# A copy moved earlier, two shortcuts at the seam between transform and MLP, a table negation deferred, and halved output tiles, in a fused Fourier-filter and MLP kernel

## The chip, the cores and the metric

The kernel runs on one core of a Trainium2 chip. The metric is the device time of one execution in microseconds (us); lower is better. The traced span (first to last instruction of the profile) is about 2 us shorter than that time, and both are given where it matters.

The engines are named as in the profile: PE is TensorE (matmuls and transposes), DVE is VectorE, ACT is ScalarE, POOL is GpSimd, SP is SyncE, which only issues transfers here.

Some words recur. An eviction copies a matmul's result out of PSUM, where TensorE leaves it, into an ordinary on-chip tile. A spill stores such a tile to the chip's main memory, and a reload brings it back. A transfer lands when its last semaphore event arrives. A launch in which two pieces of work happen to collide is called unlucky.

## The reference

```python
# x: (8, 3008, 256), filt_r and filt_i: (1505, 256)
X = np.fft.rfft(x, axis=1)
Y = X * (filt_r + 1j * filt_i)
y = np.fft.irfft(Y, n=3008, axis=1)          # 8 * 3008 = 24064 rows of 256
h = y.reshape(24064, 256) @ w_in             # w_in: (256, 2048)
g = h / (1 + np.exp(-beta * h))              # Swish with a beta for each column
out = g @ w_out                              # w_out: (2048, 256)
```

## The kernel before

The 3008 rows are split as 47 times 64, so that each transform becomes small matmuls with tables of sines and cosines. Tables `t2` (forward, second stage), `t3` and `t3b` (backward) are computed on the chip at the start. Batch 0 is transformed first, in what this text calls the head (0 to 40 us). Then the MLP starts with 752 steps, each of two 512-column matmuls into `hps`, a Swish on ScalarE and four 256-column matmuls into `acc`. The transforms of batches 1 to 7 are cut into units, and a plan places them between the steps.

These are the parts that the change touches. First the table copies in the head, issued on VectorE in program order after the evictions of column groups 3 and 4:

```python
def t2_more(h, eng):
    ks_ = slice(h * NH, (h + 1) * NH)
    nc.vector.tensor_scalar_mul(t2[:, ks_, 4, :], t2[:, ks_, 1, :], -1.0)
    eng.tensor_copy(t2[:, ks_, 3, :], t2[:, ks_, 2, :])
    eng.tensor_copy(t2[:, ks_, 0, :], t2[:, ks_, 1, :])
...
for i in range(3, 5):
    first1(i, (False, False))        # two VectorE evictions each
    warm(2)                          # two matmuls on zeros, the warm-ups
t2_more(0, nc.vector)
```

GpSimd meanwhile computes the second half of the angles: `u`, then `r` (the rounding), then `u - r` (the subtraction).

Next the product with the filter, once for each of 12 pairs of frequencies, and the backward stage of that pair. `fri` is the filter as it arrives by transfers in three groups: pairs 0 to 2, 3 to 5, and 6 to 11.

```python
def product(i):
    ...                                            # forward matmuls into ps
    for dst, ps in zip((p_t, q_t), pss):
        nc.vector.tensor_tensor(dst[:], ps[:], fri[:, 2*i : 2*i+2, :], ALU.mult)

def inverse3(i):
    ...
    last = i == NK // 2 - 1
    one = opsum.tile([P, 2, NDC, P], F32, name="psz", tag="acc")
    two = fpsum.tile([P, 2, NDC, P], F32, name="psz", tag="f") if last else one
    for e, ps in ((0, one), (1, two)):
        ...                                        # matmuls with t3 and t3b
    for e0, e1, ps in ((0, 1, one), (1, 2, two)) if last else ((0, 2, one),):
        evac(z_t[...], ps[...], e0 == 0)           # ScalarE, then VectorE
```

Then the seam: `z` is transposed (`pz`), the last stage makes `y`, and the first MLP matmul reads 512 columns of `y`. The columns are not in the natural order but in classes of `JG` = 8 residues, `CLS` = 94 * 8 = 752 columns each:

```python
def last_z(g, i, on_act, own=None):
    jq, dc = divmod(i, NDC)
    yv = ys[0][:, dc, g*CLS : (g+1)*CLS].rearrange("p (n j) -> p n j", j=JG)
    return last4(zz0[g], t4b, 4*jq, dc, yv[:, :, 4*jq : 4*jq+4], on_act, own)
...
nc.vector.tensor_scalar_mul(t3[M:P], t3b[M:P], -1.0)   # the table for batches 1 to 7
```

Last, the output: one tile of 4 x 256 columns for each block of 16 steps, two such tiles in the pool.

```python
ost = ostp.tile([P, 4, D], F32, name="ost", tag="ost")
for h, a in enumerate(acc):
    ...
    evac(ost[:, n*h : n*(h+1), :], a[:], on_act)
```

Of the kernel before, what the change touches and what calls it, by code (L numbers as in the profile page):

```python
# [9 lines left out]
P = 128  # L10
# [3 lines left out]
F32 = mybir.dt.float32  # L14
BF16 = mybir.dt.bfloat16
# [16 lines left out]
NJG = J // JG  # L32
VLAG = 3
# [3 lines left out]
def kernel(  # L37
# [23 lines left out]
    CLS = NP * JG  # L61
# [18 lines left out]
    ostp = pool("ostp", 2)  # L80
# [13 lines left out]
    t3 = consts.tile([P, NK, P], BF16, name="t3", tag="t3")  # L94
    ident = consts.tile([P, P], BF16, name="ident", tag="ident")
# [83 lines left out]
    t3b = setup.tile([P, NK, P], BF16, name="t3b", tag="t3b")  # L179
# [191 lines left out]
    for i in range(3, 5):  # L371
        first1(i, (False, False))
        warm(2)
    t2_more(0, nc.vector)
    first1(5, (True, True))
# [70 lines left out]
    def inverse3(i):  # L446
        k0 = 2 * i
        p_t, q_t = pq.pop(i)

        last = i == NK // 2 - 1  # L450
        one = opsum.tile([P, 2, NDC, P], F32, name="psz", tag="acc")
        two = fpsum.tile([P, 2, NDC, P], F32, name="psz", tag="f") if last else one
        for e, ps in ((0, one), (1, two)):
            for src, tab in ((p_t, t3), (q_t, t3b)):
                for dc in range(NDC):
                    nc.tensor.matmul(  # L456
                        ps[:, e, dc, :],
                        lhsT=src[:, e, dc * P : (dc + 1) * P],
                        rhs=tab[:, k0 + e, :],
                        start=src is p_t and dc == 0 and (e == 0 or last),  # L460
                        stop=src is q_t,
                        skip_group_check=True,
                    )
        for e0, e1, ps in ((0, 1, one), (1, 2, two)) if last else ((0, 2, one),):
            evac(
                z_t[:, :, :, 4 * (k0 + e0) : 4 * (k0 + e1)].rearrange(
                    "p c j (e a) -> p e (c j) a", a=4
                ),
                ps[:, e0:e1].rearrange("p e c (j a) -> p e (c j) a", a=4),
                e0 == 0,  # L470
            )
# [49 lines left out]

    def turn_z(g, i, on_act=False):
# [10 lines left out]
    def last4(zz, tab, jj, dc, dst, on_act, own=None):  # L533
# [10 lines left out]
        for n0, n1 in ((0, NP),) if own is None else ((0, TB // JG), (TB // JG, NP)):  # L544
# [11 lines left out]
    def last_z(g, i, on_act, own=None):  # L556
        jq, dc = divmod(i, NDC)
        yv = ys[0][:, dc, g * CLS : (g + 1) * CLS].rearrange("p (n j) -> p n j", j=JG)
        return last4(zz0[g], t4b, 4 * jq, dc, yv[:, :, 4 * jq : 4 * jq + 4], on_act, own)
# [13 lines left out]
    warm(2)  # L573
    rest = []
    for i in range(2 * NDC):
# [4 lines left out]
        if i == 1:  # L580
            warm(2)
    for go in rest:
        go()


    nc.vector.tensor_scalar_mul(t3[M:P], t3b[M:P], -1.0)
# [145 lines left out]

    def ux(b):
# [10 lines left out]
    if B > 1:  # L744
        at = place(1, 11, u1(1, True), per=2)
        place(at + 1, at + 1, [lambda: a2_read(1)] + uf(), per=9)
        at = place(25, 56, u23(1), per=2)
# [18 lines left out]
    def store(t0, tn, ost, eng=nc.sync):  # L766
# [5 lines left out]
        for tb in range(tn // P):  # L772
            c0 = t0 + tb * P
            c1 = c0 + P
            while c0 < c1:
                lo = (c0 - t0) % P
                if c0 >= S:
# [7 lines left out]
                        out.offset + (r // JG * J + g * JG) * D,  # L785
                        [[J * D, n // JG], [D, JG], [1, D]],
# [7 lines left out]
    for s in range(len(steps) + LAG):  # L794
        if s < len(steps):
# [5 lines left out]
            while pos < t0 + tn:  # L801
                b, n0 = divmod(pos, S)
                ln = min(S - n0, t0 + tn - pos)
                for dc in range(NDC):
# [16 lines left out]
        if s >= LAG:  # L821
# [26 lines left out]
            if fb == NFB - 1:  # L848
                ost = ostp.tile([P, 4, D], F32, name="ost", tag="ost")
                for h, a in enumerate(acc):  # L850
                    n = a.shape[1]
                    on_act = h == 0 and i < 6 or last and h % 2 == 0
                    evac(ost[:, n * h : n * (h + 1), :], a[:], on_act)
                    if last:
                        store(t0 + h * P, P, ost[:, h:, :], (nc.sync, nc.scalar)[h // 2])
                if not last:
                    store(t0, tn, ost)
# [30 lines left out]
```

## Time and profile before

| | before |
|---|---|
| time, median of the first 3 runs (range) | 792.48 us (791.69 to 793.87) |
| traced span | 789.8 us |
| TensorE busy | 776.7 us, 98% |
| VectorE, ScalarE, GpSimd busy | 50%, 76%, 18% |
| one MLP step in the steady state | 0.87 us |

The page of the kernel before, parts 1 and 5. Part 1 has the busy us, the share of the span and the number of instructions; part 5 has line, engine, operation, output and input, then busy us, mean ns, and idle time ahead of the group with its main releaser.

```profile
PE 776.7 (98%) x6104; PEld 547.6 (69%) x6104; DVE 396.3 (50%) x644; ACT 596.9 (76%) x920; POOL 144.6 (18%) x143
L840 PE MATMUL acc<-wout_sb,gT 128*128 128x256 bf16 x3008 | 455.1, 272 | 1.2 <-ACT ost L105 0.2
L805 PE MATMUL hps<-y,win_sb 128*128 128x512 bf16 (+7 forms) x1728 | 447.7, 351 | 0.3 <-DVE y L109 0.3
```

TensorE idles only 1.2 and 0.3 us ahead of the MLP's own matmuls. From 43 us on it is back to back apart from 1.1 us of waits (the waits view).

The head of the kernel before, the timeline of TensorE (start us, length us, engine, line, operation, count, and in brackets the idle time before it and its releaser). `pz` are the transposes of z, `hps` is the first MLP step, `acc` the first output matmuls.

```profile
37.35 1.06 PE L568 MATMUL pz<-ident,z_t 128*96 128x128 bf16 x16 [0.61 <-DVE z_t L107]
...
40.30 1.02 PE L805 MATMUL hps<-y,win_sb 128*128 128x512 bf16 x4 [0.35 <-DVE y L109]
...
42.92 0.38 PE L613 MATMUL ps<-xg,t 94*96 94x512 bf16 x1 [0.21 <-DVE a L107]
43.13 0.60 PE L840 MATMUL acc<-wout_sb,gT 128*128 128x256 bf16 x4
```

The same kernel, the timeline of VectorE: the copies, the first product of pair 6, and the negation.

```profile
13.38 0.35 DVE L290 TENSOR_SCALAR t<-t 128x768 bf16<-128x768 bf16 x1
13.64 0.98 DVE L291 COPY t<-t 128x768 bf16<-128x768 bf16 x1
14.55 1.97 DVE L292 COPY t<-t 128x768 bf16<-128x768 bf16 x1
...
27.98 0.69 DVE L443 TENSOR_TENSOR pb_t<-ps,fri 128x512 bf16<-128x512 f32 x1 [0.22 <-PE pb L396]
...
40.66 1.49 DVE L586 TENSOR_SCALAR t<-t3b 64x3072 bf16<-64x3072 bf16 x1
42.18 0.69 DVE L107 CAST a<-ps 96x512 bf16<-96x512 f32 x1
```

And the timeline of GpSimd for the same stretches.

```profile
11.60 2.81 POOL L270 TENSOR_SCALAR r<-u 128x768 f32<-128x768 f32 x1
14.49 1.80 POOL L271 TENSOR_TENSOR u<-u,r 128x768 f32<-128x768 f32 x1
...
39.44 1.89 POOL L149 TENSOR_TENSOR wout_sb<-frr,rbeta_sb 128x1024 bf16<-128x1024 f32 x1 [3.66 <-DMA frr<-in_moe_w_out_dram]
```

Three readings matter. First, the two copies of 128x768 took 0.98 and 1.97 us, although the negation of the same shape just before them took 0.35. They ended about 0.2 us after GpSimd's `r` (14.41) and its subtraction (16.29). Second, the wait before pair 6 at 27.98 is labelled with a transpose on TensorE, but the instruction also needs the filter; the transfers' semaphore events in the trace show the last of the four large filter loads landing at 27.80, so the filter was the true releaser. Third, the negation of 64x3072 took 1.49 us, ended 0.82 us after GpSimd's multiply (41.33), and held back an eviction.

### The profile page before, as it was taken

What the parts mean: (1) busy time and instruction counts of PE and PEld (TensorE: products, weight loads), DVE (VectorE), ACT (ScalarE), POOL (GpSimd) and SP (SyncE); (2) the same over time, 40 slices, a digit from 0 to 9 for tenths busy, and PEclk for the clock granted to TensorE, in tenths of its full rate; (3) what the DMA queues carried; (4) which work ended last, traced back from release to release, by engine and by line L of the source; (5) the groups of instructions that cost most, each with busy time, mean ns of one, the idle gap of its engine ahead of it and who ended that gap; (6) DMA issues with size and microseconds to landing.
All of it is one profiled execution on the core that took longest, in us unless ns stands there. A gap on an engine that the chain in (4) does not pass through costs nothing.

```text
span 789.8 us, 15387 instructions
## 1 busy us (share of the span) xinstructions
PE 776.7 (98%) x6104; PEld 547.6 (69%) x6104; DVE 396.3 (50%) x644; ACT 596.9 (76%) x920; POOL 144.6 (18%) x143
## 2 busy tenths in 40 slices
PE   7899999999999999999999999999999999999998
PEld 4767667766777667876678766686667766776665
DVE  7946935755537464465534746367452761500101
ACT  5887886886678866788677876778767788677776
POOL 9322510330013200131002310024000340000000
PEclk9999999999999999999999999999999999999999
DMA  9978687116811178011860228412370214010101
GB/s 187 232 193 213 155 212 218 49 67 187 215 45 47 68 200 218 29 68 70 216 181 28 86 97 199 152 36 88 110 222 27 74 68 127 30 52 28 54 27 53
DMA packets 83380, 91.43 MB, mean 116 GB/s; under 512 B 3759, under 2 KB 73537, under 8 KB 82287
## 3 DMA queue, kind: packets, MB, share of 16 engines
q1 hardware_dynamic: 80204, 73.95, 30.5%
q0 software_dynamic: 2816, 16.26, 10.8%
q8 instruction: 47, 0.77, 0.4%
q10 hardware_dynamic: 288, 0.26, 0.1%
q14 instruction: 25, 0.20, 0.1%
HBM read 57.16 MB, written 46.66 MB: 131 GB/s over the span
## 4 chain that ended last, share of the span: by engine, by line
PE 93%; DVE 3%; POOL 2%; issue 1%; ACT 1%; DVEq 0%; ACTq 0%; POOLq 0%
PE acc L840 41%; PE hps L805 40%; PE ps L613 3%; PE ps L536 3%; PE ps L635 2%; PE ps L661 2%; DVE ost L107 1%; PE psz L456 1%; POOL xg L116 0%; POOL r L270 0%; ACT a L105 0%; DVE q_t L650 0%; DVE p_t L646 0%; DVE q_t L647 0%; PE pt L352 0%
## 5 line engine op out<-in xcount | busy, mean ns | idle before, releaser
L814 ACT ACTIVATE gT<-hps,beta_sb 128x512 bf16<-128x512 f32 x752 | 516.8, 687 | 175.3 <-PE hps L805 165.5
L840 PE MATMUL acc<-wout_sb,gT 128*128 128x256 bf16 x3008 | 455.1, 272 | 1.2 <-ACT ost L105 0.2
L805 PE MATMUL hps<-y,win_sb 128*128 128x512 bf16 (+7 forms) x1728 | 447.7, 351 | 0.3 <-DVE y L109 0.3
L840 PEld LDWEIGHTS <-gT 128*128 128x128 bf16 x3008 | 285.3, 98 | 132.7 <-issue 4.7
L805 PEld LDWEIGHTS <-win_sb 128*128 128x128 bf16 x1728 | 164.7, 98 | 24.8 <-issue 0.7
L651 POOL TENSOR_TENSOR v_t<-p_t,q_t 128x512 bf16<-128x512 f32 x84 | 106.7, 1270 | 375.3 <-DVE q_t L650 372.7
L107 DVE COPY ost<-acc 128x512 f32<-128x512 f32 (+1 forms) x88 | 56.2, 677 | 193.6 <-PE acc L840 188.0
L107 DVE CAST a<-ps 96x512 bf16<-96x512 f32 x96 | 65.9, 686 | 85.6 <-PE ps L613 85.6
L109 DVE TENSOR_SCALAR y<-ps 128x376 bf16<-128x376 f32 (+2 forms) x120 | 64.5, 541 | 64.3 <-PE ps L536 64.2
L646 DVE TENSOR_TENSOR p_t<-ps,frr 128x512 f32<-128x512 f32 x84 | 58.1, 691 | 31.8 <-PE ps L635 29.4
L650 DVE TENSOR_TENSOR q_t<-ps,fri 64x512 f32<-64x512 f32 x84 | 58.2, 693 | 1.2
L647 DVE SCALAR_TENSOR_TENSOR q_t<-ps,fri 64x512 f32<-64x512 f32 x84 | 57.4, 684 | 1.1
L536 PEld LDWEIGHTS <-zz 96*128 96x128 bf16 x512 | 35.4, 97 | 29.0
L105 ACT ACTIVATE z<-ps 128x512 bf16<-128x512 f32 x84 | 49.5, 590 | 0.7 <-PE ps L661 0.7
L613 PE MATMUL ps<-xg,t 94*96 94x512 bf16 x112 | 41.9, 381 | 0.2 <-DVE a L107 0.2
L536 PE MATMUL ps<-t,zz 96*128 96x94 bf16 x448 | 36.7, 204 | 0.0
L116 POOL DMA_DIRECT2D xg<-in_x_dram x22 | 12.1, 556 | 114.3 <-PE acc L840 97.7
L661 PE MATMUL ps<-v_t,t 128*128 128x256 bf16 x168 | 32.1, 273 | 0.4 <-DVE q_t L650 0.4
L635 PE MATMUL ps<-a,t 128*128 128x256 bf16 x168 | 32.1, 273 | 0.0
L635 PEld LDWEIGHTS <-t 128*128 128x128 bf16 x168 | 15.8, 98 | 14.6
L613 PEld LDWEIGHTS <-t 94*96 94x96 bf16 x112 | 13.8, 123 | 12.1
L661 PEld LDWEIGHTS <-t 128*128 128x128 bf16 x168 | 15.4, 98 | 8.1 <-DVE q_t L650 0.9
(119 smaller groups left out, 201.0 us busy)
## 6 DMA issues: line engine op xcount, KB each, us to landing
out_dram<-ost SPq DMA_DIRECT2D x40, 512.0 KB, 2.8
d<-a SPq DMA_DIRECT2D x28, 384.0 KB, 4.7
a<-d SPq DMA_DIRECT2D x28, 384.0 KB, 5.8
d<-z SPq DMA_DIRECT2D x28, 384.0 KB, 2.6
zz<-d SPq DMA_DIRECT2D x28, 384.0 KB, 4.8
xg<-in_x_dram POOLq DMA_DIRECT2D x6, 1280.0 KB, 10.2
frr<-in_filt_r_dram SPq DMA_DIRECT2D x12, 256.0 KB, 7.9
out_dram<-ost SPq DMA_DIRECT2D x22, 128.0 KB, 7.1
```

The lines of the kernel that those rows point to most:

```text
L107: nc.vector.tensor_copy(dst, src)
L109: nc.vector.tensor_scalar_mul(dst, src, scale)
L536: nc.tensor.matmul(ps[:, e, :NP], lhsT=zz[:, jj + e, dc * P : (dc + 1) * P], rhs=tab[:], start=True, stop=True,)
L613: nc.tensor.matmul(ps[:KP], lhsT=t1[:], rhs=s["x"][:, 2 * i : 2 * i + 2, :], start=True, stop=True)
L635: nc.tensor.matmul(ps[:, e, :], lhsT=t2[:, k0 + e, 3:5, :].rearrange("p c k -> p (c k)"), rhs=s["a2"][g][:, kk + e, :], start=True, stop=True,
L646: nc.vector.tensor_tensor(p_t[:], ps[:], frr[:, ks_, :], ALU.mult)
L650: nc.vector.tensor_tensor(q_t[:M], ps[M:P], fri[M:P, ks_, :], ALU.mult)
L651: nc.gpsimd.tensor_tensor(v_t[:], p_t[:], q_t[:], ALU.add)
L661: nc.tensor.matmul(ps[:, e, :], lhsT=t3[:, k0 + e, :], rhs=v_t[:, e, :], start=True, stop=True)
L805: nc.tensor.matmul(hps[:, pos - t0 : pos - t0 + ln], lhsT=win_sb[:, dc, fb * P : (fb + 1) * P], rhs=ys[b][:, dc, n0 : n0 + ln], start=(dc ...
L814: nc.scalar.activation(gT[:, :tn], hps[:, :tn], ACT.Silu, scale=beta_sb[:, fb : fb + 1])
L840: nc.tensor.matmul(acc[tb // per][:, tb % per, :], lhsT=gT[:, tb * P : (tb + 1) * P], rhs=wout_sb[:, fb, :], start=(fb == 0 and tb % per = ...
```

## The change

The intent has five parts. **A**: the table copies are issued one step earlier, ahead of GpSimd's subtraction. **B**: the last pair's first columns go through the backward stage first. **C**: batch 0's `y` is kept in classes of 4 residues, so that the first 376 columns of the first MLP step need half of the evictions; three warm-up matmuls go. **D**: the table negation moves into the MLP, in four quarters, and `t3b` must then live in the constants. **E**: output tiles hold two chunks instead of four, three in the pool.

```diff
-    CLS = NP * JG
+    CLS = NP * JC                      # JC = 4                              (C)
-    ostp = pool("ostp", 2)
+    ostp = pool("ostp", 3)             #                                     (E)
+    t3b = consts.tile([P, NK, P], BF16, name="t3b", tag="t3b")   # was in setup (D)

-    for i in range(3, 5):
-        first1(i, (False, False))
-        warm(2)
+    first1(3, (False, False))
+    warm(2)
     t2_more(0, nc.vector)              #                                     (A)
+    first1(4, (False, False))
+    warm(2)

# inverse3                                                                    (B)
+        for j0, j1 in ((0, JG), (JG, J)) if last else ((0, J),):
+            ...                        # a PSUM tile for each group of columns
             for src, tab in ((p_t, t3), (q_t, t3b)):
+                for e in range(2):
                 ...
-                        rhs=tab[:, k0 + e, :],
+                        rhs=tab[:, k0 + e, 4 * j0 : 4 * j1],
+            for e in range(2) if last else (None,):
+                ...
+                evac(dst, src, not last or j0 > 0)   # first columns: VectorE

# last_z                                                                      (C)
-        return last4(zz0[g], t4b, 4*jq, dc, yv[:, :, 4*jq : 4*jq+4], on_act, own)
+        n0 = NP if jq == 0 else (TB - CLS) // JC
+        return last4(zz0[g], t4b, JC * jq, dc, yv, on_act, own, n0)
-    warm(2)
+    warm(1)
-        if i == 1:
-            warm(2)

-    nc.vector.tensor_scalar_mul(t3[M:P], t3b[M:P], -1.0)
...
+        place(14, 20, ut(4), per=2)    # the same in four quarters           (D)

# the first MLP step alone is cut at the class                                (C)
+                if s == 0:
+                    ln = min(ln, CLS - n0 % CLS)

-                ost = ostp.tile([P, 4, D], F32, name="ost", tag="ost")
                 for h, a in enumerate(acc):
+                    if h * per % 2 == 0:
+                        ost = ostp.tile([P, 2, D], F32, name="ost", tag="ost")   # (E)
```

More of the change, by code (lines that the diff above doesn't have):

```diff
@@ L32 @@
 NJG = J // JG
+JC = 4
 VLAG = 3
@@ L177, in bits @@
         return tf
-    t3b = setup.tile([P, NK, P], BF16, name="t3b", tag="t3b")
     wz = setup.tile([P, 512], BF16, name="wz", tag="wz")
@@ L450, in inverse3 @@
         last = i == NK // 2 - 1
-        one = opsum.tile([P, 2, NDC, P], F32, name="psz", tag="acc")
-        two = fpsum.tile([P, 2, NDC, P], F32, name="psz", tag="f") if last else one
-        for e, ps in ((0, one), (1, two)):
-            for src, tab in ((p_t, t3), (q_t, t3b)):
-                for dc in range(NDC):
-                    nc.tensor.matmul(
-                        ps[:, e, dc, :],
-                        lhsT=src[:, e, dc * P : (dc + 1) * P],
-                        rhs=tab[:, k0 + e, :],
-                        start=src is p_t and dc == 0 and (e == 0 or last),
-                        stop=src is q_t,
-                        skip_group_check=True,
-                    )
@@ L464, in inverse3 @@
-        for e0, e1, ps in ((0, 1, one), (1, 2, two)) if last else ((0, 2, one),):
-            evac(
-                z_t[:, :, :, 4 * (k0 + e0) : 4 * (k0 + e1)].rearrange(
-                    "p c j (e a) -> p e (c j) a", a=4
-                ),
-                ps[:, e0:e1].rearrange("p e c (j a) -> p e (c j) a", a=4),
-                e0 == 0,
-            )
+        for j0, j1 in ((0, JG), (JG, J)) if last else ((0, J),):
+            nj = 4 * (j1 - j0)
+            if j0:
+                ps = fpsum.tile([P, 2, NDC, nj], F32, name="psz", tag="f")
+            else:
+                ps = opsum.tile([P, 2, NDC, nj], F32, name="psz", tag="acc")
+            for src, tab in ((p_t, t3), (q_t, t3b)):
+                for e in range(2):
+                    for dc in range(NDC):
+                        nc.tensor.matmul(
+                            ps[:, e, dc, :],
+                            lhsT=src[:, e, dc * P : (dc + 1) * P],
+                            rhs=tab[:, k0 + e, 4 * j0 : 4 * j1],
+                            start=src is p_t and dc == 0 and e == 0,
+                            stop=src is q_t,
+                            skip_group_check=True,
+                        )
+            for e in range(2) if last else (None,):
+                if last:
+                    dst = z_t[:, :, j0:j1, 4 * (k0 + e) : 4 * (k0 + e) + 4]
+                    src = ps[:, e].rearrange("p c (j a) -> p c j a", a=4)
+                else:
+                    dst = z_t[:, :, :, 4 * k0 : 4 * k0 + 8].rearrange(
+                        "p c j (e a) -> p e (c j) a", e=2
+                    )
+                    src = ps.rearrange("p e c (j a) -> p e (c j) a", a=4)
+                evac(dst, src, not last or j0 > 0)
@@ L531, in turn_z, with last4 @@
         evac(zz0[g][:, 4 * i : 4 * i + 4, :], pz[:KP], on_act)
-    def last4(zz, tab, jj, dc, dst, on_act, own=None):
+    def last4(zz, tab, jj, dc, dst, on_act, own=None, first=NP):
         ps = own or fpsum.tile([P, 4, P], F32, name="ps4", tag="f")
@@ L543, in last4 @@
         rest = []
-        for n0, n1 in ((0, NP),) if own is None else ((0, TB // JG), (TB // JG, NP)):
+        for n0, n1 in ((0, NP),) if own is None or first == NP else ((0, first), (first, NP)):
             rest.append(
@@ L557, in last_z @@
         jq, dc = divmod(i, NDC)
-        yv = ys[0][:, dc, g * CLS : (g + 1) * CLS].rearrange("p (n j) -> p n j", j=JG)
-        return last4(zz0[g], t4b, 4 * jq, dc, yv[:, :, 4 * jq : 4 * jq + 4], on_act, own)
+        c = g * JG // JC + jq
+        yv = ys[0][:, dc, c * CLS : (c + 1) * CLS].rearrange("p (n j) -> p n j", j=JC)
+        n0 = NP if jq == 0 else (TB - CLS) // JC
+        return last4(zz0[g], t4b, JC * jq, dc, yv, on_act, own, n0)
     for i in range(4):
@@ L731, in uf, with ut @@
         ]
+    def ut(n):
+        return [
+            lambda k=k: nc.vector.tensor_scalar_mul(
+                t3[M:P, k : k + NK // n], t3b[M:P, k : k + NK // n], -1.0
+            )
+            for k in range(0, NK, NK // n)
+        ]
     def ux(b):
@@ L784, in store @@
                         out.tensor,
-                        out.offset + (r // JG * J + g * JG) * D,
-                        [[J * D, n // JG], [D, JG], [1, D]],
+                        out.offset + (r // JC * J + g * JC) * D,
+                        [[J * D, n // JC], [D, JC], [1, D]],
                     ),
@@ L848 @@
             if fb == NFB - 1:
-                ost = ostp.tile([P, 4, D], F32, name="ost", tag="ost")
                 for h, a in enumerate(acc):
-                    n = a.shape[1]
+                    if h * per % 2 == 0:
+                        ost = ostp.tile([P, 2, D], F32, name="ost", tag="ost")
+                    c = h * per % 2
                     on_act = h == 0 and i < 6 or last and h % 2 == 0
-                    evac(ost[:, n * h : n * (h + 1), :], a[:], on_act)
-                    if last:
-                        store(t0 + h * P, P, ost[:, h:, :], (nc.sync, nc.scalar)[h // 2])
-                if not last:
-                    store(t0, tn, ost)
+                    evac(ost[:, c : c + per, :], a[:], on_act)
+                    eng = nc.scalar if last and h >= 2 else nc.sync
+                    store(t0 + h * per * P, per * P, ost[:, c : c + per, :], eng)
 _INS = ['x', 'filt_r', 'filt_i', 'moe_w_in', 'moe_w_out', 'moe_beta']
```

## The prediction

> **What bounds the kernel now.** The page's busy table gives TensorE 776.7 of 789.8 us (98%). In the timeline, from 43 us on, one MLP step (two 512-column and four 256-column matmuls) repeats every 0.87 us, with side work between; the waits view shows under 1.5 us of TensorE waits after that. So only the head, 0 to 43 us, holds time that this change can win.
>
> **Step A, table copies one step earlier.** VectorE's two 128x768 bf16 copies take 0.98 and 1.97 us (0.35 each in their second half at 24.4 us). They end when GpSimd's ops end (14.41, 16.29). [...] the table negation at 40.66 ends 0.82 us after GpSimd's multiply. TensorE idles 14.4 to 16.66 waiting for these copies. Issued about 1 us earlier, they end at perhaps 13.5 to 14.7, if GpSimd's rounding (11.60 to 14.41) lets them; then up to 2 us are gained at 16.66. But I expect almost none to survive: VectorE's product of pair 6, at 27.98, waits for the four large filter loads, whose last landing in the trace is 27.80. From 27.98 to 36.18 VectorE is busy without a gap. Earlier pairs only wait there. Worth 0 to 0.2 us, estimated.
>
> **Step B, last pair's first columns first.** After the last product (36.18) the transposes start at 37.35, behind a 0.39 us ScalarE and a 0.42 us VectorE eviction of 256 elements. Then VectorE evicts two pieces of 64 elements (0.2 us each, estimated from 0.17 for 16 and 0.28 for 128): transposes at about 37.0. Gain 0.35 us.
>
> **Step C, classes of 4 residues, three fewer warm-up matmuls.** The first MLP matmul (40.30) waits for all four evictions of y, the last at 40.24. Then its 376 columns need only the first two. With 0.54 and 0.48 us for these evictions, the first MLP step ends at about 39.9 instead of 40.73: 0.8 us together with B. The ten extra small matmuls hide in waits.
>
> **Step D, negation moved.** 1.49 us of VectorE at 40.66 leave; they delayed an eviction (42.18) for which TensorE waited 0.38 us at 42.5. The four quarters (about 0.3 us each) fall at 54 to 62 us, where VectorE has idle time. Gain 0.4 us.
>
> **Step E, half output tiles.** Twice the store issues. Reuse distance falls from two blocks to one and a half, about 14 us instead of 28 from eviction to reuse; stores land in 2.8 to 7 us, latest for block 0 (issued at 68 to 72, evicted at 61). 0, with a small risk around 80 us. The tail is unchanged.
>
> **Sum.** Estimated 1.2 us of the head, plus 0 to 0.2 from A: **791.1 us**, range 789.5 to 792.4. Chances: faster by over 2% 0.01, within 2% 0.98, slower by over 2% 0.01.
>
> **What would show it.** A: transposes of the first table well before 16.66, yet VectorE's pair 6 still at about 27.9 with a wait before it of 1 to 2 us. B: transposes of z at about 37.0. C: first MLP matmul at about 39.4, first SiLU at about 40.1 (was 40.93). D: no wait before the third stage-1 matmul after the first steps; from there all MLP steps about 1.2 us earlier, unchanged to the end.
>
> **What would make it wrong.** The big filter loads landing earlier or later (then A counts); the copies still blocked, with two evictions now behind them; transposes waiting for the second column group; an output eviction waiting for a store; run-to-run scatter (2.2 us over three runs of before) is as large as the effect.

0.8 us from B and C and 0.4 us from D make the 1.2 us, with 0 to 0.2 us from A on top.

## The result, and the profile after

| | before | after |
|---|---|---|
| time, median of 6 runs (range) | 792.33 us (791.69 to 793.87) | 790.63 us (790.00 to 792.63) |
| ratio, with its 95% interval | | 0.9978 (0.9964 to 0.9993) |
| traced span | 789.8 us | 788.4 us |
| TensorE busy | 776.7 us | 777.5 us |

A ratio here is the mean time of one kernel's fast runs over that of the kernel before in the same rounds, so it is not quite the ratio of the medians quoted.

The page of the kernel after, part 1 and the same two groups:

```profile
PE 777.5 (99%) x6111; PEld 547.9 (69%) x6111; DVE 394.4 (50%) x647; ACT 597.4 (76%) x920; POOL 144.6 (18%) x143
L860 PE MATMUL acc<-wout_sb,gT 128*128 128x256 bf16 x3008 | 455.1, 272 | 1.2 <-ACT ost L107 0.2
L825 PE MATMUL hps<-y,win_sb 128*128 128x512 bf16 (+8 forms) x1730 | 447.7, 351 | 0.0
```

The MLP itself costs the same 455.1 and 447.7 us. The timeline of TensorE in the head of the kernel after:

```profile
36.06 1.06 PE L581 MATMUL pz<-ident,z_t 128*96 128x128 bf16 x16 [0.19 <-DVE z_t L109]
...
38.26 1.04 PE L825 MATMUL hps<-y,win_sb 128*128 128x376 bf16 x6
...
40.74 0.60 PE L860 MATMUL acc<-wout_sb,gT 128*128 128x256 bf16 x4
```

From the first `pz` to the first `hps` it is now 2.20 us (2.95 before), and the wait before `pz` is 0.19 us (0.61 before). The timeline of VectorE for the kernel after:

```profile
12.36 0.35 DVE L291 TENSOR_SCALAR t<-t 128x768 bf16<-128x768 bf16 x1
12.63 0.35 DVE L292 COPY t<-t 128x768 bf16<-128x768 bf16 x1
12.90 0.35 DVE L293 COPY t<-t 128x768 bf16<-128x768 bf16 x1
...
27.01 0.69 DVE L446 TENSOR_TENSOR pb_t<-ps,fri 128x512 bf16<-128x512 f32 x1 [0.64 <-PE ps L437]
```

The timeline of GpSimd for the kernel after:

```profile
11.61 2.81 POOL L271 TENSOR_SCALAR r<-u 128x768 f32<-128x768 f32 x1
```

The copies now take 0.35 us each, in the middle of GpSimd's `r`. Yet VectorE then stands idle before pair 6 (0.64 us): the filter landed at 26.83, and pair 6 started 0.18 us later. Pair 6 is 0.97 us earlier than in the trace of before, and the first temptation is to credit that to A. The filter loads were not touched by A, though. On the other hand, VectorE itself was ready for pair 6 only at 27.76 in the trace of before (27.98 less 0.22), so with copies held up as there, the earlier landing alone could have gained no more than 0.22 us. The experiments had to say whose gain this was.

The two traces, cut at the same events, add up exactly. Positive numbers are time lost by the kernel after:

| stage | before | after | difference |
|---|---|---|---|
| start of pair 6 | 27.98 | 27.01 | -0.97 |
| pair 6 to the end of the last product | 8.19 | 8.19 | 0 |
| end of products to first transpose of z (B) | 1.18 | 0.86 | -0.32 |
| first transpose of z to first MLP matmul (C) | 2.95 | 2.20 | -0.75 |
| first MLP matmul to first output matmul (D) | 2.83 | 2.48 | -0.35 |
| first output matmul to Swish 4 (counted from 0) | 2.74 | 2.73 | -0.01 |
| Swish 4 to 42 | 42.52 | 42.53 | +0.01 |
| Swish 42 to 52 | 12.06 | 12.30 | +0.24 |
| Swish 52 to 83 | 33.82 | 33.86 | +0.04 |
| Swish 83 to 90 | 6.77 | 7.19 | +0.42 |
| Swish 90 to 751 | 643.60 | 643.59 | -0.01 |
| last Swish to the end | 5.18 | 5.44 | +0.26 |
| sum | 789.82 | 788.39 | -1.43 |

So 2.4 us were gained up to Swish 4, and about 0.95 us were given back later in four places of which the prediction named none.

### The profile page after: what moved, and what is told of

The parts are those of the page before. It is cut to its first block, busy times and chain, and to the rows that moved or that the text cites. A ratio compares the mean times of both kernels' runs of the same rounds, so it can differ in the third digit from the quotient of the medians.

```text
span 788.4 us, 15540 instructions
## 1 busy us (share of the span) xinstructions
PE 777.5 (99%) x6111; PEld 547.9 (69%) x6111; DVE 394.4 (50%) x647; ACT 597.4 (76%) x920; POOL 144.6 (18%) x143
## 4 chain that ended last, share of the span: by engine, by line
PE 90%; DMA 5%; DVE 3%; issue 1%; POOL 0%; DVEq 0%; ACT 0%; POOLq 0%; SPq 0%; ACTq 0%
PE acc L860 40%; PE hps L825 39%; PE ps L621 3%; PE ps L546 2%; PE ps L643 2%; PE ps L669 2%; DMA fri<-in_filt_i_dram 1%; DMA d<-a 1%; DVE ost L109 1%; DMA xg<-in_x_dram 1%; DMA mark<-xg 1%; DMA a<-d 0%; DVE qb_t L446 0%; DVE q_t L658 0%; DVE pb_t L446 0%
## 5 line engine op out<-in xcount | busy, mean ns | idle before, releaser
L860 PE MATMUL acc<-wout_sb,gT 128*128 128x256 bf16 x3008 | 455.1, 272 | 1.2 <-ACT ost L107 0.2
L825 PE MATMUL hps<-y,win_sb 128*128 128x512 bf16 (+8 forms) x1730 | 447.7, 351 | 0.0
L111 DVE TENSOR_SCALAR y<-ps 128x376 bf16<-128x376 f32 (+1 forms) x119 | 64.4, 545 | 63.1 <-PE ps L546 62.9
```

The lines of the kernel that those rows point to most:

```text
L111: nc.vector.tensor_scalar_mul(dst, src, scale)
L825: nc.tensor.matmul(hps[:, pos - t0 : pos - t0 + ln], lhsT=win_sb[:, dc, fb * P : (fb + 1) * P], rhs=ys[b][:, dc, n0 : n0 + ln], start=(dc ...
L860: nc.tensor.matmul(acc[tb // per][:, tb % per, :], lhsT=gT[:, tb * P : (tb + 1) * P], rhs=wout_sb[:, fb, :], start=(fb == 0 and tb % per = ...
```

## The experiments

Every experiment was timed beside runs of the kernel before, and traced once. Twelve kernels were run. Their times (medians; n is the number of runs of the kernel itself):

| run | edit | time, us | n | before, us | ratio (95%) |
|---|---|---|---|---|---|
| before_again | none | 792.42 | 6 | 792.43 | 1.0003 (0.9986 to 1.0019) |
| after_again | none | 790.60 | 5 | 792.43 | 0.9977 (0.9965 to 0.9989) |
| copies_only | before + A | 791.86 | 6 | 792.43 | 0.9993 (0.9978 to 1.0008) |
| no_copies | after - A | 791.08 | 6 | 792.43 | 0.9984 (0.9966 to 1.0002) |
| copies_late | before, copies forced late | 792.95 | 4 | 793.12 | 1.0002 (0.9977 to 1.0027) |
| after_no_late_filter | after, wrong result | 791.13 | 4 | 793.12 | 0.9981 (0.9955 to 1.0006) |
| filter_later | after, MLP's filter loads later | 790.55 | 6 | 793.12 | 0.9991 (0.9955 to 1.0026) |
| split_and_later | filter_later + head's loads split | 789.45 | 6 | 793.12 | 0.9955 (0.9931 to 0.9979) |
| negate_back | after - D | 791.10 | 4 | 792.33 | 0.9981 (0.9958 to 1.0005) |
| pairs_back | after - B | 791.79 | 4 | 792.33 | 0.9991 (0.9968 to 1.0014) |
| best | split_and_later + denser plan | 788.96 | 6 | 792.33 | 0.9955 (0.9938 to 0.9972) |
| best_tail | best + five tiny writes | 788.79 | 6 | 792.33 | 0.9951 (0.9935 to 0.9967) |

One launch of a kernel differs from the next by about 1 us either way (with single runs up to 8 us above their median), which is as much as the whole effect. A part of 0.3 us cannot be read from these times. It can be read from traces, because the same two events in two traces are often a constant distance apart. The head in ten traces (us from the span's start; the three last columns are differences):

```
kernel         filter   pair 6  products  first  first   first   products  pz to  hps to
               landed   starts  end       pz     hps     acc     to pz     hps    acc
before         27.80    27.98   36.17     37.35  40.30   43.13   1.18      2.95   2.83
before_again   27.58    27.76   35.96     37.13  40.08   42.54   1.17      2.95   2.46
copies_late    27.70    28.42   36.84     38.01  40.96   43.42   1.17      2.95   2.46
copies_only    27.15    27.33   35.53     36.70  41.29   44.69   1.17      4.59   3.40  (clock halved)
after          26.83    27.01   35.20     36.06  38.26   40.74   0.86      2.20   2.48
after_again    27.42    27.59   35.79     36.65  38.85   41.33   0.86      2.20   2.48
no_copies      26.24    26.41   34.61     35.47  37.67   40.15   0.86      2.20   2.48
filter_later   27.17    27.35   35.54     36.40  38.60   41.07   0.86      2.20   2.47
negate_back    26.92    27.10   35.29     36.16  38.36   40.83   0.87      2.20   2.47
pairs_back     27.19    27.37   35.57     36.74  38.94   41.41   1.17      2.20   2.47
```

And what came after it, Swish numbers from 0, in us, with TensorE's wait near 51 us (the distance between two starts, less what the matmuls between them take; a dash where it was not read):

```
kernel                4 to 42  42 to 52  52 to 83  83 to 90  90 to 751  last to end  wait near 51
before                 42.52    12.06     33.82     6.77      643.60     5.18         0
before_again           42.52    12.06     33.82     6.77      643.61     5.18         -
after                  42.53    12.30     33.86     7.19      643.59     5.44         0
after_again            42.74    12.29     33.87     7.77      643.61     5.43         0.23
no_copies              43.73    12.30     33.86     7.52      643.61     5.44         1.22
negate_back            43.34    12.31     33.87     7.25      643.61     5.43         0.81
pairs_back             42.83    12.30     33.87     6.77      643.61     5.43         0
after_no_late_filter   47.02    12.30     33.87     7.36      643.60     5.44         2.84 (and clock halved)
filter_later           42.52    12.30     33.86     6.77      643.60     5.43         0
split_and_later        42.53    12.30     33.86     9.39      643.60     5.44         0
best                   42.52    12.24     34.39     6.77      643.63     5.56         0
best_tail              42.52    12.24     34.14     6.77      643.89     5.13         0
```

The 42.83 us of pairs_back are no wait: its Swish 4 alone ran 0.3 us early. From Swish 5 to 42 it took 41.29 us, as after did, and TensorE had no idle time near 51 us.

### before_again and after_again: how much is chance?

No edit. These two traces show what differs between two launches of one kernel.

> The kernel before once more, for the scatter of one trace to the next. If the late filter loads decide when VectorE's product of pair 6 starts, its start follows their last landing within 0.2 us (27.80 and 27.98 in the first trace). Landings may differ by about 1 us between traces; if instead they repeat within 0.3 us, then the change itself made them 1 us earlier in the trace of after. Ratio to before 1.000.

> The changed kernel once more. First trace: last filter landing 26.83, pair 6 at 27.01, first SiLU at 38.90, a wait of 0.40 us near 132 us for the reload of batch 2. If the landing is chance, it lies anywhere from 26.8 to 27.8 here, and the first SiLU moves with it; if the change moved it, it repeats at 26.8. Ratio to before 0.998.

The times repeated (792.42 and 790.60), but the traces did not. The second trace of before has a span of 789.24 and the second of after 789.78, so this pair of traces would have said that the change costs 0.54 us, where the first pair said that it gains 1.43. Cut at the same stages: pair 6 -0.17, B -0.31, C -0.75, D +0.02, and then +0.22, +0.23, +0.05, +1.00, 0.00 and +0.25 later. B and C are the same in both pairs. The start of pair 6, D, and the give-backs are not.

The timeline of VectorE in the second trace of before shows why D differs, and that even A's blocking is chance:

```profile
12.82 0.36 DVE L291 COPY t<-t 128x768 bf16<-128x768 bf16 x1
13.09 0.36 DVE L292 COPY t<-t 128x768 bf16<-128x768 bf16 x1
...
27.76 0.69 DVE L443 TENSOR_TENSOR pb_t<-ps,fri 128x512 bf16<-128x512 f32 x1 [3.01 <-PE ps L434]
...
40.44 1.08 DVE L586 TENSOR_SCALAR t<-t3b 64x3072 bf16<-64x3072 bf16 x1
```

The copies are in the old place in this program and still took 0.36 us each. The third load of x, on which the evictions ahead of them hang, landed at 9.65 us in the first trace of before, at 8.28 in this one and at 8.41 in no_copies, which has the old order too and was not blocked. So the copies seem to slip into GpSimd's way when this load is late; three traces suggest it, no run sets it alone. And although VectorE was then 3.01 us ahead of the filter, pair 6 started at 27.76, as late as in the first trace: the time won by unblocked copies was absorbed in front of pair 6.

### copies_only and no_copies: what is A worth?

```diff
 # copies_only: the kernel before, with A's reordering and nothing else
-    for i in range(3, 5):
-        first1(i, (False, False))
-        warm(2)
+    first1(3, (False, False))
+    warm(2)
     t2_more(0, nc.vector)
+    first1(4, (False, False))
+    warm(2)
 # no_copies: the reverse of this edit, in the kernel after
```

> Only the two table copies moved ahead (nothing else of the change). Theory (late filter loads absorb it): the first table transposes start at about 14.1 instead of 16.66, but pair 6 starts at the last filter landing, so the first SiLU comes 0 to 0.2 us earlier than in a trace of before with the same landing, up to 1 us earlier in all. Rival (the step is worth its 2.5 us): first SiLU at about 38.5. Time ratio 0.9985 to 1.0.

> The whole change but the copies, which stay where they were. Theory: copies blocked again until 16.5, pair 6 at about 27.9, last pair, classes and negation give 1.4 us at the second MLP weights: first SiLU at about 39.9, and the third stage-1 matmul without its wait. Ratio 0.998 to 0.9995. If the copies gave most of the gain, the ratio is 1.0.

Neither time is told apart from that of its neighbour: 0.9993 for A alone, and 0.9984 for everything but A against 0.9977 for everything. In the traces pair 6 started 0.18 us after the landing of the filter with A (27.15 to 27.33) and 0.17 us without it (26.24 to 26.41). The earliest pair 6 of the ten is one without A. This supports the reading that time won by A is absorbed in front of the filter.

It doesn't settle A, for no_copies missed its expectation: the copies were not blocked. The timeline of VectorE of no_copies:

```profile
12.90 0.35 DVE L292 COPY t<-t 128x768 bf16<-128x768 bf16 x1
13.17 0.35 DVE L293 COPY t<-t 128x768 bf16<-128x768 bf16 x1
```

So no trace here joins blocked copies to a filter that landed early. An estimate: VectorE was ready at 27.76 in the first trace of before, where the copies were blocked. Blocked in the same way, with the filter landing as in after (pair 6 at 27.01) or as in no_copies (26.41), pair 6 would come 0.75 or 1.35 us later. The 0.97 us of the first pair of traces thus needed the earlier landing, and may have needed A as well.

The trace of copies_only fell on something else, so what was expected of its first Swish (it came at 41.92 us) can't be judged. The windows view of that run has, for each stretch (us from the span's start), its length, busy time and count of PE, PEld (weight loads), DVE, ACT and POOL, the granted clock of TensorE, the transfers' share and GB/s:

```profile
34.00:36.00 2.00, 1.28 (x16) 0.79 (x14) 1.53 (x3) 1.12 (x3) 1.32 (x1) 1.00 1.00 203
36.00:38.00 2.00, 1.39 (x17) 1.33 (x16) 0.84 (x2) 0.70 (x2) 0.57 (x1) 0.73 1.12 248
38.00:40.00 2.00, 2.00 (x15) 1.28 (x14) 0.81 (x2) 0.85 (x3) 0.00 (x0) 0.50 1.00 193
40.00:42.00 2.00, 1.65 (x14) 0.89 (x13) 1.19 (x5) 1.09 (x5) 1.00 (x1) 0.91 0.99 205
```

TensorE's granted clock was 0.5 for about 3.4 us from about 36.9 us on (the means of 0.73, 0.50 and 0.91 add up to that), so transposes and last stage took 4.59 instead of 2.95 us (the 16 transposes alone 1.70 instead of 1.06). What brought this on is not shown: from 30 to 36 us TensorE was busy for 4.72 us here and for 4.73 us in before_again, where the clock stayed at 1.00. The halved clock is one reason why single traces of the head must not be compared whole.

### after_no_late_filter: is the filter the bound in the head?

Pairs 6 to 11 take the filter of pairs 0 to 5, which is there long before. The result is wrong (relative error 0.357); the amount of work is the same.

```diff
-            nc.vector.tensor_tensor(dst[:], ps[:], fri[:, 2 * i : 2 * i + 2, :], ALU.mult)
+            j = 2 * i % (2 * KG)
+            nc.vector.tensor_tensor(dst[:], ps[:], fri[:, j : j + 2, :], ALU.mult)
```

> The changed kernel, wrong on purpose: pairs 6 to 11 multiply by the first half of the filter, so they don't wait for the late loads. Theory: VectorE has no wait before pair 6, which starts 0.6 us or more earlier than 0.18 us after the last landing, at about 26.2; first SiLU at about 38.1 (38.9 and 39.5 in the two traces of after). Rival (something else holds pair 6): start still 0.17 us after the landing or with another wait, first SiLU unchanged. In all the ratio may stay at 0.998 if the first spill of the MLP, which waits for transfers, takes the gain back at 52 us.

Pair 6 started at 25.27 with no wait, 1.47 us ahead of the landing (26.74), and the first MLP matmul at 36.52 instead of 38.26. So the wait in front of pair 6 is the filter, and with unblocked copies nothing else is close behind it: shown. The median nevertheless did not fall (791.13). The traced run (793.10) loses 2.84 us near 51 us and then runs at half clock for 3.4 us (a granted clock of 0.50 at 54 to 56 us and of 0.66 at 56 to 58 us); the other three (790.57 to 791.28, mean clock 1.000) were not traced. The loss near 51 us is the next wait in the line, taken up under filter_later.

### copies_late: can A ever matter?

The kernel before, with four small writes on VectorE ahead of the copies, so that they meet GpSimd every time.

```diff
+    late = setup.tile([P, 256], F32, name="late", tag="late")
+    for _ in range(4):
+        nc.vector.memset(late[:], 0.0)
     t2_more(0, nc.vector)
```

> The kernel before, with four memsets (about 1.1 us of VectorE) ahead of the table copies, so that the copies always meet GpSimd's subtraction, as in the first trace of before. Theory (late filter loads absorb it): copies end at about 16.5, first table transposes at about 16.7 (13.6 in the second trace of before), yet pair 6 starts 0.2 us after the last filter landing (26.2 to 27.8 in six traces) or at most at 28.0, and first SiLU stays at 40.3 to 41.2. Rival (the copies are on the path): first SiLU 2.5 to 3 us later than in the second trace of before, near 43.5; ratio 1.003.

The timeline of VectorE in this run:

```profile
13.56 1.45 DVE L376 MEMSET late<- 128x256 f32 x4
14.92 1.60 DVE L290 TENSOR_SCALAR t<-t 128x768 bf16<-128x768 bf16 x1
16.44 0.35 DVE L291 COPY t<-t 128x768 bf16<-128x768 bf16 x1
...
27.82 0.68 DVE L446 TENSOR_TENSOR qb_t<-ps2q,fri 128x512 bf16<-128x512 f32 x1
28.42 0.68 DVE L446 TENSOR_TENSOR pb_t<-ps,fri 128x512 bf16<-128x512 f32 x1
```

The four small writes took 1.45 us beside GpSimd (1.1 us were expected; one write of this size takes 0.27 us in the trace of before). The negation after them was held up more: it took 1.60 us instead of 0.35 and ended 0.2 us after GpSimd's subtraction (16.31). By which mechanism is not shown. Pair 6 now starts at 28.42 without a wait: VectorE is late, not the filter (27.70). So blocked copies can reach the critical path, but here by only about 0.5 us (28.42 against 27.70 + 0.18 = 27.88). The expectation that the filter would hide the delay, with pair 6 no later than 28.0, missed by this 0.4 us. The rival, in which the delay reaches the MLP in full, fell as well: the copies and the table after them were 3.8 us later than in before_again (first table transpose at 17.41 against 13.59), and the first MLP matmul only 0.88 us (40.96 against 40.08). The time is not distinguished (1.0002). A is therefore insurance against an unlucky launch: worth about 0.5 us in this one, nothing in the first trace of before, and up to 1.35 us by the estimate above if the filter lands early. Nor does it always avoid GpSimd: in five traces with A the negation ahead of the copies started at 11.63 to 12.10 and was held until 12.64 or 12.65; in three of them VectorE then waited for the filter anyway. When GpSimd starts to hold VectorE up can't be read from a trace: its `r` is reported from 11.61 us on both in negate_back, where the negation at 11.63 took 1.02 us instead of 0.35, and in after, where the copies at 12.63 and 12.90 took 0.35 us each.

### negate_back: what is D worth?

The kernel after, with the negation back at its place in front of the MLP.

```diff
+    nc.vector.tensor_scalar_mul(t3[M:P], t3b[M:P], -1.0)
     sp.close()
 ...
-        place(14, 20, ut(4), per=2)
```

> The changed kernel with the table negation back before the MLP. Prediction's step D: TensorE waits about 0.4 us again ahead of the third stage-1 matmul; from the first MLP matmul to the first output matmul 2.8 us (2.83 before, 2.48 after). Rival (it only fills a gap): 2.48 stays. Time 0.2 to 0.4 us over after, within noise.

From the first MLP matmul to the first output matmul it took 2.47 us with the negation and 2.48 without. The expected cost of 0.4 us did not show. The timeline of VectorE in this run:

```profile
38.88 0.96 DVE L596 TENSOR_SCALAR t<-t3b 64x3072 bf16<-64x3072 bf16 x1
39.87 0.69 DVE L109 CAST a<-ps 96x512 bf16<-96x512 f32 x1
```

And that of GpSimd in the same run:

```profile
39.50 2.09 POOL L151 TENSOR_TENSOR wout_sb<-frr,rbeta_sb 128x1024 bf16<-128x1024 f32 x1 [3.94 <-DMA frr<-in_moe_w_out_dram]
```

Here GpSimd's multiply started after the negation and was the one that was delayed (2.09 us instead of 1.89), while the negation took 0.96 us, as in copies_late, where the multiply had ended. In the first trace of before the multiply started first, the negation took 1.49 us, and TensorE waited. In before_again the multiply ended at 40.69, 0.25 us after the negation's start; the negation took 1.08 us and cost nothing (2.46). When the multiply starts depends on the landing of `w_out` (GpSimd waited 3.66 us for it in before, 3.94 in negate_back). In copies_only they collided again (2.06 us, ended 0.82 us after the multiply), but the halved clock hides the cost. So D was worth 0.37 us in the one unlucky launch in which it can be read, and nothing in three others.

### pairs_back: what are B and C worth?

The kernel after, with the old order in the backward stage (the reverse of B's part of the diff).

> The changed kernel with the last pair (and the order of the matmuls in all pairs) as before. Prediction's step B: from the end of the last product to the first transpose of z 1.18 us again (0.86 in after); the order within the other pairs changes nothing, since VectorE sets their pace: pair 9 still 4.06 us after pair 6. Time about 0.3 us over after, within noise.

The distance from the end of the products to the first transpose went back from 0.86 to 1.17 us, and that from there to the first MLP matmul stayed at 2.20. So B is 0.31 to 0.32 us and C is 0.75 us, each a constant over all the traces in the table above (apart from the one with the halved clock), and B's part is still there at Swish 42. No run undoes C, and C is two edits in one, the classes and three warm-up matmuls fewer. In the trace of before two of the warm-ups held TensorE for 0.43 us (38.25 to 38.68), so three are some 0.64 us (an estimate), of which a part may hide in waits. How the 0.75 us split between the two edits is not shown. The new order of matmuls within the other eleven pairs, which comes with B, changed nothing: pair 6 to pair 9 took 4.06 us with and without it.

### filter_later: the wait near 51 us

In the kernel after, the first four loads of the MLP's filter (256 KB each) are issued after the first spill of batch 1 instead of ahead of it.

```diff
-    for at in (0, M):
-        for go in load_filter(frr, filt_r, at, 0, JG, nc.sync):
-            go()
 ...
         place(at + 1, at + 1, [lambda: a2_read(1)] + uf(), per=9)
+        place(4, 4, uf(0, JG), per=9)
```

> The changed kernel, with the first 1 MB of the MLP's filter loads behind the first spill of stage 1 instead of ahead of it. Theory: the spill was issued at 43.2 to 44.6 and waited behind 1 MB of loads; now it lands before 49 us and the TensorE wait at 51 to 52 us (0, 0.23 and 1.22 us in three traces with the new classes) is gone in every trace; from the 4th to the 42nd MLP step 42.5 us (42.53, 42.75, 43.73 before). Rival (the wait has another cause): it stays. Ratio 0.997 to 0.998. New risk: the filter's loads late for the first product at about 66 us.

The wait is best seen where it was largest among the kernels without a wrong result, in no_copies. The timeline of VectorE of no_copies:

```profile
47.05 0.69 DVE L109 CAST a<-ps 96x512 bf16<-96x512 f32 x1 [0.55 <-PE ps L619]
51.85 1.28 DVE L109 CAST a<-ps 96x512 bf16<-96x512 f32 x2 [4.11 <-DMA d<-a]
```

And the timeline of TensorE of no_copies:

```profile
52.59 0.33 PE L544 MATMUL ps<-t4b,zz 96*128 96x94 bf16 x4 [1.05 <-DVE a L109]
```

VectorE cannot evict into `a` until the spill of the first `a` tile has landed, and that landed between 50.5 and 52.2 us in the traces in which VectorE waited for it, behind the filter loads. How long TensorE waits follows from both ends, the finish of the head and the landing: not at all in before, nor in after (landed at 50.54), 0.23 us in after_again (51.92), 1.22 in no_copies (51.73), whose head was the earliest of the ten. A gain in the head can thus be partly taken back 10 us later. The timeline of VectorE of filter_later shows the same eviction with its ordinary releaser, and the one after it:

```profile
50.38 0.69 DVE L109 CAST a<-ps 96x512 bf16<-96x512 f32 x1 [1.71 <-PE ps L618]
51.63 0.69 DVE L109 CAST a<-ps 96x512 bf16<-96x512 f32 x1 [0.56 <-PE ps L618]
```

With the loads behind the spill it lands at 45.4 to 47.6 us, and the wait is gone in this trace, in split_and_later, in best and in best_tail (Swish 4 to 42 is 42.52 or 42.53 us in all four): shown. The timed ratio (0.9991) has one run at 798.79 us in it and says nothing; its median is 790.55.

### split_and_later: both waits taken away

In addition the head's filter loads are issued in smaller groups, in the order in which they are used (frequencies 2, 4, 6, 6 and 6 instead of 6, 6 and 12).

```diff
-    FG = ((0, KG), (KG, KG), (2 * KG, 2 * KG))
+    FG = ((0, 2), (2, KG - 2), (KG, KG), (2 * KG, KG), (3 * KG, KG))
 ...                                    # the loop issues the groups in order
```

> As filter_later, and the filter of the setup loaded in five groups (2, 4, 6, 6, 6 of the 24) instead of three (6, 6, 12), so that pair 0 waits for 2 rows and pair 6 for half as much. Theory: VectorE's first product 0.5 to 1 us earlier (about 16.2), no wait for loads before pair 6 (at about 25.5), first SiLU at about 37.3 to 38.2, nothing given back at 52 us. Ratio 0.996. If VectorE is not held by landings there, first SiLU as in after (38.9 to 39.5).

Pair 6 started at 25.07 without a wait, the first MLP matmul at 36.55, and the time fell to 789.45 us. The trace also shows where the next piece went. The timeline of TensorE of split_and_later:

```profile
132.82 0.38 PE L638 MATMUL ps<-a,t 128*128 128x256 bf16 x2 [2.46 <-DMA a<-d]
```

The same place in the kernel after, timeline of TensorE:

```profile
132.33 0.38 PE L643 MATMUL ps<-a,t 128*128 128x256 bf16 x2 [0.26 <-DMA a<-d]
```

This is the reload of batch 2's first stage. Its last spill is queued on SyncE behind output stores. The classes of 376 columns cut a block of 512 rows in more places than classes of 752, so five stores stood ahead of that spill where before had four. In the first trace of after they were issued from 114.22 to 117.9 us, and the spill landed at 128.31. TensorE waited 0.42 us in after, 1.00 in after_again, 2.6 here, and not at all in before, pairs_back and filter_later. The stores ahead of the spill don't explain these differences: the spill landed 3.5 to 4.0 us before Swish 83 in all of them, in before too. What differs is how long the first part of the reload took from its issue: 3.2 to 3.3 us in the three without a wait, 3.90 in after, 4.15 in after_again, 5.76 here. Why it took longer is open.

### best and best_tail: a version that beats both

best gives batch 2's first stage fewer steps, so that its spill starts earlier. best_tail adds five writes of 64 bytes in the middle of the MLP, which do no work.

```diff
 # best
-        at = place(50, 66, u1(2, True), per=3)
+        at = place(50, 62, u1(2, True), per=3)
 # best_tail, in addition
+        for n in range(5):
+            c = slice(n * 32, (n + 1) * 32)
+            place(400 + n, 400 + n, [lambda c=c: nc.sync.dma_start(mark[:, c], win_sb[:1, 0, c])])
```

> split_and_later, with the stage-1 work of batch 2 packed into 13 MLP steps instead of 17, so that its last spill leaves ahead of the five output stores and the load of batch 3. Theory (the reload of batch 2 waits for that spill, which was issued behind the stores): the last spill is issued at about 111 instead of 116.3, and the TensorE wait at 130 us (0.43, 1.0, 0.75 and 2.6 us in four traces) is gone: from the 83rd to the 90th MLP step 6.77 us. Last SiLU at about 780.8 (783.44 in split_and_later), span 786.3, ratio 0.993 to 0.995. Rival (bandwidth, not order): the wait shrinks by less than half.

> As best, with five tiny writes to scratch in the middle of the MLP, which only turn the order of the transfer queue's semaphores so that the last output store ends on the last of them. Theory (the end waits for the eight semaphores in a fixed order, 0.063 us each, and in the changed kernel five satisfied ones come after the last landing, in before one): from last SiLU to the end 5.1 us instead of 5.44. Rival (half tiles make the last stores slower): 5.44 stays. The ratio to best is too small to time.

In best the spill was issued at 110.27 us (116.29 in split_and_later) and landed 6.4 us before Swish 83 instead of 3.5. The stretch from Swish 83 to 90 is back at 6.77 us in best and best_tail, at a cost of 0.3 to 0.5 us in the denser stretch before it. The timeline of TensorE of best:

```profile
131.09 0.38 PE L638 MATMUL ps<-a,t 128*128 128x256 bf16 x2
```

So an earlier spill takes the wait away, though the reload's first part was also shorter in best (3.39 us), and two kernels without this edit had no wait either. The expected last Swish (780.8) and ratio (0.993 to 0.995) were missed: 781.75 and 0.9955. The times of best and best_tail are 788.96 and 788.79 us against 792.33: ratios of 0.9955 and 0.9951, intervals wholly below 1 and below the median of after.

The five writes concern the tail. The last instructions wait for the eight transfer semaphores of the stores, always in the same order, and each wait that is already satisfied still takes about 0.061 us (0.304 us for five in after). In before, one of these waits follows the last landing (788.84 us). The change alters the number of transfers, the semaphores are dealt out in turn (the last four stores of before landed, at 787.82 to 788.84 us, on four that stand next to each other in the order of the waits), and in after five waits follow the last landing (787.17 us). From last Swish to the end it was 5.18 us in before, 5.43 to 5.44 in eight traces of kernels with the change, 5.56 in best and 5.13 in best_tail, whose five writes turn the count on until no wait follows the last landing (785.63 us): shown. The time itself does not tell best_tail from best (788.79 and 788.96), and 0.26 us were lost between Swish 90 and 751, where the five writes stand.

### What could not be tried

The kernel after with full output tiles (without E) is not among the runs: by the author's report it did not build, for want of on-chip space. What E is for is thus the author's reading, which no run shows: D moves `t3b` (24 x 128 bf16, 6 KB for each partition) from the setup's space, which is given back, to the constants, which are not; the half tiles make room for it.

## Why the prediction was right or wrong

The predicted 791.1 us (789.5 to 792.4) contains the measured 790.63. The total was right; several of its terms were not, and that they added up to it is in part luck, as the end of this section says.

- **What bounds the kernel: right.** The MLP's 455.1 and 447.7 us did not move, and every difference found in the traces is in the head, in waits before 133 us, or in the tail.
- **Step A, 0 to 0.2 us: its mechanism right, its size not settled.** Pair 6 starts 0.17 or 0.18 us after the filter's last landing in all nine traces in which VectorE was ahead of it, with and without A. Taking the filter's wait away moved pair 6 to 25.27. But in the first trace of after the filter landed 0.97 us earlier than in before, the case for which the prediction had said "then A counts": up to 0.75 us of it may be A's (the estimate above), and no run separates them. What was not foreseen is that A's blocking itself is chance: before_again ran the old order unblocked.
- **Step B, 0.35 us: right.** It measured 0.31 to 0.32 us, in every comparison and by undoing it.
- **Step C, "0.8 us together with B": mechanism right, size off.** C alone measured 0.75 us (classes and fewer warm-ups together), so B and C together are 1.07 us. The mis-sized term was the first MLP step: the prediction put its Swish at about 40.1 us (0.8 us earlier); with the filter's landing taken out it came 1.06 us earlier (40.93 - 27.98 = 12.95 us after pair 6 before, 38.90 - 27.01 = 11.89 us after).
- **Step D, "Gain 0.4 us": failed.** The 0.38 us of waiting were real in the one trace that the prediction had, and came from a collision of the negation with GpSimd's multiply. In before_again, negate_back and copies_late the negation was in the same place and cost nothing; in copies_only it collided again. The step that failed was to take one trace's collision as the rule. The four quarters took 0.36 us each in the trace of after (52.0 to 62.2 us), where about 0.3 had been estimated.
- **Step E, "0 ... the tail is unchanged": right on reuse, wrong on the tail, and blind to its purpose.** No output eviction waited for a store. The tail grew by 0.25 us through the order of the final waits, and E's purpose is the space for `t3b` (the author's reading, as said above).
- **"all MLP steps about 1.2 us earlier, unchanged to the end": failed.** Relative to the start of pair 6, the kernel after reaches Swish 4 1.05 us earlier than before_again (17.52 us before_again, 16.46 us after). Then, against before_again, 0.96 us (after) or 1.76 us (after_again) are given back: 0 to 0.23 us near 51 us, and up to 1.22 in no_copies (first spill behind the filter loads, shown by filter_later), 0.23 to 0.24 us at Swish 42 to 52, 0.42 to 1.00 us near 132 us (a slower reload, of open cause; best shows that an earlier spill avoids it), and 0.25 us in the tail (shown by best_tail). The 0.23 us are only argued: TensorE waited there for VectorE's `q_t` (0.24 us at 88.70 us in after, a wait that the trace of before does not have); that another rotation of PSUM buffers causes it is the author's reading, and no run undid it.

With so much given back, why is the time still 1.7 us shorter? Not all of it is explained. About 0.5 us lie outside the traced span: time minus span is 1.76 to 1.88 us in the 11 runs of after, and 2.18 to 2.43 us in the 11 runs of before beside them. It is 1.99 to 2.04 us in pairs_back, 1.76 to 1.88 in no_copies, 1.76 to 1.83 in negate_back and 2.26 to 2.47 in copies_only, so it goes with B and with C or E, which no run separates; its cause was not found. Inside the span the medians differ by 1.2 us (790.0 and 788.8 over 11 runs each), which is more than B and C less the give-backs. What may make up the rest is the landing of the filter: 27.15 to 27.80 us in the four traces of kernels with the old seam, 26.24 to 27.42 in the seven with the new one and unsplit loads. The groups overlap, nothing in the changed parts is known to act on those loads, and the earliest landing came in the run without A. The expectation had called it an effect of the change if the landings of before repeated within 0.3 us; they did (27.80 and 27.58), but that of after did not (26.83 and 27.42). Whether this is chance or an effect of the change stays open.

## What to carry to other kernels

Before an earlier start is counted as a gain, follow it to the next thing that does not move with it: a load's landing absorbed time won before it (VectorE stood 3.01 us ahead of it in before_again), and a spill's landing and a reload took back part of B and C (up to 1.22 us and 0.42 to 1.00 us). A collision seen in one trace is one draw; take a second trace of the unchanged kernel before giving its cost to a step, and compare distances between two events rather than ends of traces. When a wait's label names an engine that had long been done, look for the transfer that landed last. On top of the five edits (ratio 0.9978), moving and splitting such transfers, with a denser plan, brought the kernel to 0.9955 (best), about as much again.
